# VectorE in place of GpSimd for the low parts of a feed-forward layer's weights

## The chip, the cores and the metric

The kernel runs on one core of a Trainium2 chip. The metric is the device time of one execution in microseconds (us); less is better. Three runs of the kernel before gave 726.19, 727.13 and 728.55 us, so the median is 727.13.

The engines are named as the profile names them: PE is TensorE's matmul, PEld its weight load, DVE is VectorE, ACT is ScalarE, POOL is GpSimd, SP is SyncE, whose queue issues nearly all DMAs.

## The reference

Three layers follow each other on 2 x 576 = 1152 tokens of width 512, all in float32:

```python
x = gate * memory(q) + (1 - gate) * causal_attention(q, k, v)   # 8 heads of 64
r = np.maximum(x @ w_in, 0.0); x = (r * r) @ w_out              # 512 -> 2048 -> 512
p = domain_probs / domain_probs.sum(-1, keepdims=True)
out = sum(p[:, e:e+1] * (np.maximum(x @ w1[e], 0.0) @ w2[e]) for e in range(4))
```

The first feed-forward layer (`w_in`, `w_out`) is the one that the change touches.

## The kernel before, in words

**Tiles and chunks.** The 1152 tokens are nine tiles of 128. The attention and the first feed-forward layer go through them in three chunks (`CHUNKS`, L38): chunk 0 has two tiles, chunk 1 four (512 columns), chunk 2 three (384 columns). The chunks of the layer overlap with the attention of what comes later: while the layer works on chunk 0 the attention of chunk 1 runs beside it, while it works on chunk 1 the attention of chunk 2 runs beside it (`mix`, L822; in the profile about 100 to 281 us), and while it works on chunk 2 (about 281 to 362 us) the weights and tokens of the experts are prepared (L1013 to L1027). Then come the experts, to the end.

**The weights of the layer.** `convert` writes the layer's weights into a DRAM buffer `w1s` during chunk 0: 16 blocks `f`, each with a half 0 (of `w_in`) and a half 1 (of `w_out`), 128 x 512 float32 each. Chunks 1 and 2 read all 32 halves back, each chunk for itself. To keep precision every product is made of three passes (`PASS`, L41): a weight is split into a high part in the narrower format `F32R` and a low part, the rest. High times high, high times low and low times high are added up.

**One block, step by step.** `prep(f, half)` (L725) does this for chunks 1 and 2: `fetch` (L719) sees to it that a DMA of the half into a tile `wraw` is under way (L723, three buffers); `split` (L82) makes the high part with a copy on ScalarE (L83), and the low part as `raw` minus the high part (L84), on VectorE or on GpSimd; then `fetch(2)` asks for the next half. The engine of L84 is chosen at L735: in chunk 1, VectorE makes half 0 of blocks 0 to 2 and half 1 of blocks 3, 7, 11 and 15; in chunk 2 half 1 of the odd blocks. That is 15 of 64; GpSimd makes the other 49, 25 in chunk 1 and 24 in chunk 2.

`up(f)` (L740) multiplies the tokens by half 0 (L106, 12 matmuls into `hpb` in chunk 1, `hpc` in chunk 2), then ScalarE takes the relu (L745), VectorE multiplies it by the same bank again, which gives the square `r` (L746), ScalarE copies its high part (L751) and VectorE makes its low part `g` (L752). `down(f)` (L755) multiplies by half 1 (L762, 12 matmuls). The loop (L774) preps half 0 of block f+1 and half 1 of block f-1, then runs `up(f)` and `down(f-2)`. In chunk 1 all `up` write into one bank but for one block, so the next `up` waits until L746 has read it; chunk 2 has two banks.

**What lies beside it.** In chunk 1 `attention_b` gives VectorE most of its work: L189 (masked scores and their maximum), L573 and L574 (the exponential's bias), L588 and L589 (high and low part of the exponentials), L511, L516, L530, L183 and L184 (keys, queries and values in parts). GpSimd makes the other keys' low parts (also L511). In chunk 2 VectorE has L873 and L890 (the experts' tokens) and L928 (the experts' weights), and GpSimd L931 to L936 (sums of the experts' weights). ScalarE also takes the squares of the experts' weights (L869), and SP issues their loads (L917).

**What sets the order.** The program order of PE is fixed by the source. The queues of the other engines are put in order by the framework's planner, from the program order and from when it expects each operand to be ready. Each engine works through its queue in that order.

Of the kernel before, what the change touches and what calls it, by code (L numbers as in the profile page):

```python
# [52 lines left out]
def attention_then_experts(ctx, tc, qa, ka, va, qc, kc, vc, mz, beta, w1, probs, w2, out):  # L53
# [11 lines left out]
    nc = tc.nc  # L65
# [16 lines left out]
    def split(w, raw, eng):  # L82
        nc.scalar.activation(out=w[:, 0], in_=raw, func=AF.Copy)  # L83
        eng.tensor_sub(w[:, 1], raw, w[:, 0].bitcast(F32))  # L84

    def y_of(c):

        t0 = CHUNKS[c][0]
        if t0 < LAST and 0 not in ys:
            ys[0] = xyp.tile([P, NK, LAST * P], F32, tag=f"x{c}", name="y0")  # L90
        e = int(t0 >= LAST)
        t0 -= EXPERT_CHUNKS[e][0]
        return ys[e][:, :, t0 * P:t0 * P + (CHUNKS[c][1] - CHUNKS[c][0]) * P]
# [3 lines left out]
    def mm_in(c, acc, w):  # L97
        i = 0
        for kk in range(NK):
            if c == 0:  # L100
                nc.tensor.matmul(
                    acc, lhsT=w[:, kk * P:(kk + 1) * P], rhs=first_x[:, kk, :],
                    start=(kk == 0), stop=(kk == NK - 1),
                )
            for a, b in PASS if c else ():
                nc.tensor.matmul(  # L106
                    acc, lhsT=w[:, a, kk * P:(kk + 1) * P], rhs=xs_r[c][:, b, kk, :],
                    start=(i == 0), stop=(i == 3 * NK - 1),
                )
                i += 1  # L110
            yield
# [598 lines left out]
    def ffn1(c, ps, gp, nh, cv=None):  # L710
        t0, t1 = CHUNKS[c]
        n = (t1 - t0) * P
        per = 512 // n
        gs, ws = {}, {}

        todo = [x for g in range(n1 + 1) for x in ((g, 0), (g - 2, 1)) if 0 <= x[0] < n1] + [(n1 - 1, 1)]
        raws = {}

        def fetch(ahead):  # L719
            while c and todo and len(raws) < ahead:  # L720
                x = todo.pop(0)
                raws[x] = wrp.tile([P, DM], F32, tag="wraw", name="wraw")
                nc.sync.dma_start(out=raws[x], in_=w1s[x])  # L723

        def prep(f, half):  # L725
            if c == 0:
                while (f, half) not in made:
                    next(cv)
                ws[f, half] = made.pop((f, half))
                next(cv, None)  # L730
                return
            fetch(1)
            raw = raws.pop((f, half))
            w = wp.tile([P, 2, DM], F32R, tag=f"w{half}", name=f"w{half}")
            on_vector = ((f < 3, f % 4 == 3), (False, f % 2))[c - 1][half]  # L735
            split(w, raw, nc.vector if on_vector else nc.gpsimd)
            ws[f, half] = w
            fetch(2)

        def up(f):  # L740
            spare = c == 1 and f == 1
            hp = (ps if spare or f % nh else ps_h).tile([P, n], F32, tag="s" if spare else "h", bufs=2 if spare else 1, name="hp" + "abc"[c])
            yield from mm_in(c, hp, ws.pop((f, 0)))
            r = gp.tile([P, n], F32, tag="r", name="r") if c else gp.tile([P, n], F32, tag="g", name="g0", bufs=3)
            nc.scalar.activation(out=r, in_=hp, func=AF.Relu)  # L745
            nc.vector.scalar_tensor_tensor(out=r, in0=hp, scalar=0.0, in1=r, op0=ALU.max, op1=ALU.mult)  # L746
            if c == 0:
                gs[f] = r
                return
            g = gp.tile([P, 2, n], F32R, tag="g", name="g", bufs=3)  # L750
            nc.scalar.activation(out=g[:, 0], in_=r, func=AF.Copy)  # L751
            nc.vector.tensor_sub(g[:, 1], r, g[:, 0].bitcast(F32))  # L752
            gs[f] = g

        def down(f):  # L755
            w, g = ws.pop((f, 1)), gs.pop(f)
            for d in range(NK):
                first, last = f == 0 and d % per == 0, f == n1 - 1 and d % per == per - 1
                if c == 0:
                    nc.tensor.matmul(yacc[d], lhsT=w[:, d * P:(d + 1) * P], rhs=g, start=first, stop=last)  # L760
                for i, (a, b) in enumerate(PASS if c else ()):
                    nc.tensor.matmul(  # L762
                        yacc[d], lhsT=w[:, a, d * P:(d + 1) * P], rhs=g[:, b],
                        start=(first and i == 0), stop=(last and i == 2),
                    )
                for k in range(d - per + 1, d + 1) if last else ():
                    nc.scalar.activation(out=y_of(c)[:, k], in_=yacc[k], func=AF.Copy)
                yield

        prep(0, 0)  # L770
        ps = (yield) or ps
        banks = [ps.tile([P, per, n], F32, tag=f"y{d}", name=f"y{d}") for d in range(NK // per)]
        yacc = [banks[d // per][:, d % per, :] for d in range(NK)]
        for f in range(n1 + 2):  # L774
            if f + 1 < n1:
                prep(f + 1, 0)
            if 1 <= f <= n1:
                prep(f - 1, 1)
            if f < n1:
                yield from up(f)  # L780
            if f >= 2:
                yield from down(f - 2)
        for k in range(NK):
            junk = gp.tile([P, n], F32, tag="r", name="junk")
            nc.scalar.activation(out=junk, in_=y_of(c)[:, k], func=AF.Square, accum_out=ysq[:, c, k:k + 1])
# [382 lines left out]
```

## Time and profile before

| what | before |
|---|---|
| median of three runs | 727.13 us |
| the profiled execution's own time | 726.71 us |
| its span, first to last instruction | 724.9 us |
| PE busy | 679.4 us (94%) |
| VectorE busy | 548.1 us (76%) |
| ScalarE busy | 428.2 us (59%) |
| GpSimd busy | 239.3 us (33%) |
| mean granted clock of TensorE | 0.991 of full speed |

The profile is of one execution; its span is 1.8 us shorter than that execution's own time. Busy time is what the engine's instructions took; the share is of the span. A line such as L84 is a line of the kernel. A busy PE isn't PE at its peak, since matmuls are pipelined and their ends modelled.

### The profile page before, as it was taken

Reading aid. Unit: us, or ns where it says so; the run is one execution under the profiler, and the core shown is the slowest. Engines: PE = TensorE matmul, PEld = TensorE weight load, DVE = VectorE, ACT = ScalarE, POOL = GpSimd, SP = SyncE. Lnnn points to the kernel's source line nnn. Section 1 sums busy time; section 2 is a strip of 40 time slices with the busy share of each in tenths; the row PEclk is TensorE's granted clock in tenths of the full one; section 3 lists DMA queues with packets and bytes.
Section 4 is the critical chain, followed back from the end, with each engine's and each line's share of the span. In section 5 each row is a group of like instructions: output and inputs, shape, how many; then the busy total and the mean of one; then the engine's idle time right before and its main releaser. Section 6 shows DMA issues by size and latency. Waiting matters only on the chain.

```text
span 724.9 us, 12553 instructions
## 1 busy us (share of the span) xinstructions
PE 679.4 (94%) x4604; PEld 482.5 (67%) x4604; DVE 548.1 (76%) x1058; ACT 428.2 (59%) x842; POOL 239.3 (33%) x247
## 2 busy tenths in 40 slices
PE   7799899988999999989899999999999999999997
PEld 4577677766777778989665655666655555555553
DVE  7888776499979853667788778998787785867763
ACT  5888894666665546877786667455544343535340
POOL 1011003245242365545524423544332323242400
PEclk9999999999999999999999999999999999999999
DMA  8987983468875554875321322333333131100002
GB/s 304 343 312 234 305 259 91 172 214 208 192 172 118 126 108 125 284 247 156 103 89 59 117 84 92 117 117 117 115 118 117 60 113 62 59 1 1 1 1 72
DMA packets 65422, 101.25 MB, mean 140 GB/s; under 512 B 32656, under 2 KB 34704, under 8 KB 65360
## 3 DMA queue, kind: packets, MB, share of 16 engines
q1 hardware_dynamic: 65216, 100.45, 45.2%
q8 instruction: 36, 0.59, 0.3%
q14 instruction: 26, 0.21, 0.1%
q10 hardware_dynamic: 144, 0.00, 0.0%
HBM read 82.87 MB, written 10.75 MB: 129 GB/s over the span
## 4 chain that ended last, share of the span: by engine, by line
PE 51%; DVE 19%; ACT 12%; DMA 7%; issue 6%; POOL 3%; SPq 0%; DVEq 0%; ACTq 0%; POOLq 0%
PE o L1056 19%; PE pe L964 16%; DMA raw<-in_w 4%; PE y L762 4%; PE hpb L106 3%; PE y L760 2%; PE pv L619 2%; ACT a L319 2%; DMA wraw<-w1s 2%; DVE wu L928 2%; DVE g L752 1%; DVE a L189 1%; DVE w L873 1%; PE sc L551 1%; DVE g L980 1%
## 5 line engine op out<-in xcount | busy, mean ns | idle before, releaser
L1056 PE MATMUL o<-w,g 128*128 128x512 f16 x864 | 218.3, 379 | 6.9 <-DVE g L980 3.6
L964 PE MATMUL pe<-xs,wu 128*128 128x256 f16 (+1 forms) x1344 | 196.3, 286 | 1.9 <-DVE h L985 1.9
L964 PEld LDWEIGHTS <-wu 128*128 128x128 f16 x1344 | 131.0, 98 | 69.9 <-issue 3.5
L1056 PEld LDWEIGHTS <-g 128*128 128x128 f16 x864 | 83.8, 98 | 77.2 <-DVE g L980 6.6
L84 POOL TENSOR_TENSOR w<-wraw,w 128x512 fp32r<-128x512 f32 x49 | 72.5, 1484 | 144.6 <-ACT w L83 144.2
L979 ACT ACTIVATE g<-h 128x512 f16<-128x512 f32 (+1 forms) x64 | 43.3, 677 | 105.7 <-DVE h L985 105.7
L762 PE MATMUL y<-g,w 128*128 128x512 f32 (+1 forms) x384 | 90.7, 372 | 1.7 <-ACT w L83 0.9
L994 POOL TENSOR_TENSOR u<-u,p 128x256 f32<-128x256 f32 (+1 forms) x32 | 32.4, 1012 | 131.9 <-ACT p L993 111.0
L762 PEld LDWEIGHTS y<-g,w 128*128 128x128 f32 x384 | 68.2, 189 | 9.9 <-ACT w L83 1.2
L980 DVE SCALAR_TENSOR_TENSOR g<-h,g 128x512 f16<-128x512 f32 (+1 forms) x64 | 50.5, 788 | 25.5 <-ACT g L979 25.2
L985 DVE SCALAR_TENSOR_TENSOR h<-pe,u 128x256 f32<-128x256 f32 (+1 forms) x96 | 42.9, 452 | 19.8 <-PE pe L964 15.7
L106 PE MATMUL hpb<-x,w 128*128 128x512 f32 x192 | 53.2, 414 | 4.7 <-DVE r L746 4.6
L931 POOL TENSOR_TENSOR ws<-raw 128x256 f32<-128x256 f32 x32 | 23.3, 728 | 102.0 <-issue 79.8
L928 DVE SCALAR_TENSOR_TENSOR wu<-ws,wpow,wu 128x512 f16<-128x512 f32 x64 | 50.9, 835 | 2.9 <-ACT wu L939 2.9
L873 DVE SCALAR_TENSOR_TENSOR w<-raw,wpow,w 128x512 f16<-128x512 f32 x64 | 48.1, 755 | 0.7 <-ACT w L872 0.6
L83 ACT ACTIVATE w<-wraw 128x512 fp32r<-128x512 f32 x64 | 39.6, 622 | 14.9 <-DMA wraw<-w1s 8.4
L869 ACT ACTIVATE junk<-raw 128x1024 bf16<-128x1024 f32 x32 | 33.6, 1050 | 20.6 <-DMA raw<-in_w 20.5
L106 PEld LDWEIGHTS hpb<-x,w 128*128 128x128 f32 x192 | 36.3, 196 | 13.7 <-DVE r L746 6.5
L872 ACT ACTIVATE w<-raw,wpow 128x512 f16<-128x512 f32 x64 | 44.6, 709 | 0.9 <-PE o L1056 0.9
L106 PE MATMUL hpc<-x,w 128*128 128x384 f32 x192 | 37.9, 341 | 4.0 <-POOL w L84 3.1
L189 DVE CUSTOM_DVE_ANT_0 a<-sc,mask 128x384 f32<-128x384 f32 (+4 forms) x80 | 35.7, 477 | 5.5 <-PE sc L551 5.1
L752 DVE TENSOR_TENSOR g<-r,g 128x512 fp32r<-128x512 f32 (+1 forms) x32 | 30.7, 961 | 10.4 <-ACT g L751 9.8
(169 smaller groups left out, 1164.4 us busy)
## 6 DMA issues: line engine op xcount, KB each, us to landing
raw<-in_w SPq DMA_DIRECT2D x64, 512.0 KB, 3.4
w<-in_w SPq DMA_DIRECT2D x32, 512.0 KB, 5.3
wraw<-w1s SPq DMA_DIRECT2D x64, 256.0 KB, 3.0
w1s<-bits SPq DMA_DIRECT2D x32, 256.0 KB, 3.2
kraw<-in_kc SPq DMA_DIRECT2D x8, 576.0 KB, 4.1
vraw<-in_vc SPq DMA_DIRECT2D x8, 320.0 KB, 4.1
qraw<-in_qc SPq DMA_DIRECT2D x4, 512.0 KB, 4.7
out<-acc SPq DMA_DIRECT2D x8, 256.0 KB, 2.1
```

Of the source, the lines that this page charges most:

```text
L84: eng.tensor_sub(w[:, 1], raw, w[:, 0].bitcast(F32))
L106: nc.tensor.matmul(acc, lhsT=w[:, a, kk * P:(kk + 1) * P], rhs=xs_r[c][:, b, kk, :], start=(i == 0), stop=(i == 3 * NK - 1),)
L189: nc.vector.tensor_tensor_reduce(out=dst, in0=sc, in1=msk, op0=ALU.add, op1=ALU.max, scale=1.0, scalar=-3.0e38, accum_out=m)
L762: nc.tensor.matmul(yacc[d], lhsT=w[:, a, d * P:(d + 1) * P], rhs=g[:, b], start=(first and i == 0), stop=(last and i == 2),)
L872: nc.scalar.activation(out=w0, in_=x, func=AF.Copy, scale=s)
L873: nc.vector.scalar_tensor_tensor(out=w1, in0=x, scalar=s, in1=w0, op0=ALU.mult, op1=ALU.subtract)
L928: nc.vector.scalar_tensor_tensor(out=w[:, 1, ks], in0=x, scalar=s1, in1=w[:, 0, ks], op0=ALU.mult, op1=ALU.subtract)
L964: nc.tensor.matmul(acc, lhsT=w[:, wa, k, kk * P:kk * P + P], rhs=x[:, xb, kk], start=(m == 0), stop=(m == 5))
L979: nc.scalar.activation(out=g[:, 0], in_=hm, func=AF.Relu)
L980: nc.vector.scalar_tensor_tensor(out=g[:, 1], in0=hm, scalar=0.0, in1=g[:, 0], op0=ALU.max, op1=ALU.subtract)
L985: nc.vector.scalar_tensor_tensor(out=out, in0=acc, scalar=HID, in1=x, op0=ALU.mult, op1=ALU.add)
L1056: nc.tensor.matmul(outs[t], lhsT=g[:, gb, r:r + P], rhs=w[:, wa], start=(p == 0 and m == 1 and k == 0), stop=(p == 3 and m == 0 and k == 2),)
```

## The change

All 64 subtractions of L84 go to VectorE, whatever the chunk, block and half. Nothing else is edited.

```diff
             w = wp.tile([P, 2, DM], F32R, tag=f"w{half}", name=f"w{half}")
-            on_vector = ((f < 3, f % 4 == 3), (False, f % 2))[c - 1][half]
-            split(w, raw, nc.vector if on_vector else nc.gpsimd)
+            split(w, raw, nc.vector)
             ws[f, half] = w
```

## Rows read from the trace of the kernel before

**Rows 1.** Busy time by stretch: window, length, busy per engine (instructions), PE's clock, DMA share, GB/s

```profile
140.00:190.00 50.00, 43.75 (x229) 34.05 (x228) 47.91 (x66) 32.99 (x60) 26.35 (x16) 0.93 0.82 220
190.00:250.00 60.00, 58.70 (x455) 46.09 (x454) 52.20 (x95) 34.57 (x73) 19.88 (x14) 1.00 0.66 146
281.00:322.00 41.00, 37.76 (x209) 35.73 (x210) 25.66 (x40) 35.15 (x71) 19.34 (x15) 1.00 0.77 263
```

**Rows 2.** The same stretches, L84 alone: VectorE, then GpSimd

```profile
140.00:190.00 50.00, 0.69 (x1) 16.24 (x10) 0.93 0.82 220
```

**Rows 3.** Line L84 in the whole run: shortest, median, longest ns, first and last start

```profile
L84 POOL TENSOR_TENSOR w<-wraw,w x49: 1276/1301/2507, 110.1 to 351.2; 128x512 fp32r<-128x512 f32 x49
L84 DVE TENSOR_TENSOR w<-wraw,w x15: 678/693/1532, 106.0 to 356.8; 128x512 fp32r<-128x512 f32 x15
```

**Rows 4.** Instructions in order of time, chunk 1: start, duration, engine, line

```profile
145.36 1.69 POOL L84 TENSOR_TENSOR w<-wraw,w 128x512 fp32r<-128x512 f32 x1 [1.31 <-ACT w L83]
145.84 1.76 DVE L752 TENSOR_TENSOR g<-r,g 128x512 fp32r<-128x512 f32 x1
...
148.25 4.62 PE L106 MATMUL hpb<-x,w 128*128 128x512 f32 x12 [3.44 <-DVE r L746]
...
187.39 0.68 DVE L752 TENSOR_TENSOR g<-r,g 128x512 fp32r<-128x512 f32 x1
```

**Rows 5.** Groups by line and form, VectorE, 140 to 250 us: count, busy us, mean ns

```profile
L752 DVE TENSOR_TENSOR g<-r,g 128x512 fp32r<-128x512 f32 x14 | 15.0, 1072 | 2.2 <-ACT g L751 2.2
L589 DVE TENSOR_TENSOR al<-a,ah 128x1024 f16<-128x1024 f32 x7 | 12.6, 1806 | 0.0
...
L573 DVE TENSOR_TENSOR mx<-mx 128x2 f32<-128x2 f32 x3 | 1.7, 569 | 0.1
```

**Rows 6.** Three VectorE lines in the whole run: shortest, median, longest ns

```profile
L589 DVE TENSOR_TENSOR al<-a,ah x12: 1212/1358/2345, 163.7 to 267.6; 128x1024 f16<-128x1024 f32 x8, 128x1152 f16<-128x1152 f32 x4
L573 DVE TENSOR_TENSOR mx<-mx x4: 161/163/1382, 177.6 to 262.4; 128x2 f32<-128x2 f32 x4
L746 DVE SCALAR_TENSOR_TENSOR r<-hpb,r x16: 677/686/694, 137.4 to 268.8; 128x512 f32<-128x512 f32 x16
```

**Rows 7.** Groups by line and form, GpSimd, 140 to 250 us

```profile
L84 POOL TENSOR_TENSOR w<-wraw,w 128x512 fp32r<-128x512 f32 x21 | 31.8, 1513 | 59.7 <-ACT w L83 59.4
L511 POOL TENSOR_TENSOR kst<-kraw,kst 64x576 fp32r<-64x576 f32 x8 | 14.5, 1827 | 14.1 <-ACT kst L509 12.6 <-issue 1.4
```

**Rows 8.** Groups by line and form, VectorE and GpSimd, 281 to 362 us

```profile
L752 DVE TENSOR_TENSOR g<-r,g 128x384 fp32r<-128x384 f32 x16 | 13.3, 832 | 7.5 <-ACT g L751 6.9 <-PE wt L851 0.6
L84 DVE TENSOR_TENSOR w<-wraw,w 128x512 fp32r<-128x512 f32 x8 | 7.8, 980 | 4.3 <-ACT w L83 4.1
...
L84 POOL TENSOR_TENSOR w<-wraw,w 128x512 fp32r<-128x512 f32 x21 | 29.6, 1422 | 34.0 <-ACT w L83 34.0
```

**Rows 9.** Waits: PE 140 to 285 us; PE 284 to 400; SP 284 to 345 (total, times, longest)

```profile
PE hpb L106 <- DVE r L746: 4.6, 2, 3.4
...
PE hpc L106 <- POOL w L84: 3.1, 4, 1.2
...
PE y L762 <- POOL w L84: 0.7, 1, 0.7
...
SPq L723 <- POOL w L84: 32.4, 18, 4.0
```

**Rows 10.** Instructions in order of time, chunk 2: two of PE's waits for GpSimd's L84

```profile
306.84 1.28 POOL L84 TENSOR_TENSOR w<-wraw,w 128x512 fp32r<-128x512 f32 x1 [2.71 <-ACT w L83]
...
307.45 1.21 DVE L84 TENSOR_TENSOR w<-wraw,w 128x512 fp32r<-128x512 f32 x1 [1.10 <-ACT w L83]
...
308.17 2.02 PE L106 MATMUL hpc<-x,w 128*128 128x384 f32 x10 [0.74 <-POOL w L84]
...
312.42 0.68 DVE L890 TENSOR_TENSOR tt<-y 128x512 f32<-128x512 f32 x1
...
314.28 2.00 PE L106 MATMUL hpc<-x,w 128*128 128x384 f32 x10 [1.18 <-POOL w L84]
```

## The prediction

> **What bounds the kernel now.** Read first the table of busy time by stretch, to see which engine is full where the change acts. It acts in two places. From 140 to 250 us the first layer's chunk 1 runs beside the attention of chunk 2. There VectorE is busy 47.9 of the first 50 us, while PE has 43.8; in the next 60 us PE has 58.7 and VectorE 52.2 [rows 1]. So VectorE sets the pace first, PE later. From 281 us on, in chunk 2, VectorE is busy only 25.7 of 41 us and PE 37.8 [rows 1]: there PE waits for operands. Read second the waits. Up to 285 us PE waits 4.6 us for L746, a VectorE instruction, and never in the leading rows for GpSimd's L84; after 284 us it waits 3.1 + 0.7 = 3.8 us, five times, for L84 on GpSimd [rows 9]. So the moved work is off PE's path in chunk 1 and on it in chunk 2.
>
> Read third what GpSimd does to VectorE. In order of time, at 145.36 us an L84 begins on GpSimd and runs 1.69 us; L752, begun beside it on VectorE, takes 1.76 us, where the same instruction took 0.68 us at 187.39 [rows 4]. The one is stretched by 1.08 us. L746 is not: its longest is 694 ns against 677 for its shortest [rows 6]. It is the one that reads one of its inputs from PE's bank.
>
> **The change, part by part.** *Which instructions move.* 49 subtractions leave GpSimd, 15 are on VectorE already [rows 3]. By time, 10 of the 49 lie between 140 and 190 us [rows 2], 21 between 140 and 250 [rows 7], 21 between 281 and 362 [rows 8]; the other seven lie around these, where I cost them at nothing: of what is left of chunk 1, VectorE's work is the thin end. One costs 0.69 us on VectorE, the median, against 1.30 on GpSimd [rows 3]. No DMA moves: the loads of `wraw` stay in SP's queue, in the same order.
>
> *What VectorE gains and loses in chunk 1.* Added: 21 x 0.69 = 14.5 us. Taken away: the stretch. In the groups of VectorE between 140 and 250 us, eleven have a mean far over their own fastest. The first is L752, 14 x (1.072 - 0.68) = 5.5 us [rows 4, 5]; the second L589, 7 x (1.806 - 1.212) = 4.2 [rows 5, 6]; the last L573, 3 x (0.569 - 0.161) = 1.2 [rows 5, 6]. With the eight between (L589's wider form, L530, L511, L574, two forms of L588, L184, L516), each against its own fastest, it comes to some 23 us. GpSimd spends 31.8 us of that stretch in L84 and 14.5 in L511 [rows 7], and L511 stays. By these shares 31.8 / 46.3 x 23 = 15.8 us would go. VectorE's net is 14.5 - 15.8 = -1.3 us. As VectorE is full for less than half of the stretch, I take 0 on the path. The bounds: nothing comes back, which puts 10 x 0.69 = 6.9 us on the path where VectorE is full; or all of it comes back early enough to take away PE's 4.6 us of waits for L746.
>
> A rule speaks against this move. The Trainium skill, in "Perfetto Trace Analysis", section Optimizing Scalar/DVE Operations, says that work may be offloaded from a saturated VectorE, even to GpSimd, but that the two share a read port, so that moving work between them might not help. By its first half the sum would be 726.7 + 6.9 - 2.7 = 730.9 us, by its second the term of chunk 1 is about nothing. The stretched L752 [rows 4] speaks for the second half.
>
> *What PE gains in chunk 2.* Five waits, 3.8 us [rows 9]. In the first one shown, L84 starts on GpSimd at 306.84 and ends at 308.12; VectorE is idle until 307.45 and could end it at 306.84 + 0.69 = 307.53, which saves 0.6 us. In the second, VectorE is in L890 until 313.10 and would end at 313.79, where PE went on at 314.28: 0.5 us [rows 10]. At 0.55 us each the five give 2.7 us. The bounds are nothing and the whole 3.8.
>
> *What VectorE bears in chunk 2.* Added 21 x 0.69 = 14.5 us. Its own eight L84 now take 0.980 us on the mean, against 0.678 at the fastest, so 2.4 us come back there [rows 3, 8]. L752 takes 0.832 on the mean [rows 8]; it is 384 columns wide and so should take under 0.6 (an estimate from the 0.68 at 512 [rows 4]), which gives another 16 x 0.23 = 3.7. The net is about +8.4 us. It is covered by 41 - 25.7 = 15.3 us in which VectorE is idle in the first part of this chunk alone [rows 1]. Without that cover it would cost the 8.4.
>
> *What comes earlier.* SP waits 32.4 us, 18 times, for L84 on GpSimd before it can issue the next `wraw` load [rows 9], since L84 is the last reader of that buffer. A shorter L84 lets it go sooner. I give that nothing, because DMAs are already busy 0.77 of the time in that stretch [rows 1]; it may help to make the 2.7 us stick.
>
> *The sum.* The profiled execution took 726.7 us (span 724.9, 1.8 around it); 726.7 + 0 - 2.7 = 724.0. The median of the runs is 0.4 above that execution, so 724.4 us, 0.37% less. About 0.3%, or 2.2 us, is what a measurement of this kernel can tell from no change.
>
> **The rivals.** *No difference that shows.* In chunk 2 each L84 stands behind a ScalarE copy and a DMA. VectorE's own L84 waited 4.1 us for L83 there [rows 8], and ScalarE is at 35.2 of 41 us [rows 1]. If PE's five waits pass to those, perhaps 0.7 us is left: 726.0, or 726.4 at the median. Against it: in the rows PE stands still to the end of GpSimd's own instruction.
>
> *Slower: the subtraction blocks VectorE's queue.* GpSimd now waits 59.4 us for L83 between 140 and 250 us and 34.0 after 281 [rows 7, 8]; it has little behind. On VectorE what stands behind is L746, for which PE already waits up to 3.4 us [rows 9]. The eight L84 of chunk 2 on VectorE had 4.3 us of idle time before them, 0.54 each [rows 8]. At half of it, 21 x 0.27 = 5.7 us come into chunk 1, less the 1.3 of relief 4.4, and in chunk 2 the full 0.54 eats the 0.55 saved. This gives 726.7 + 4.4 = 731.1, or 731.5 at the median. It turns the sign from (1.3 + 2.7) / 42 = 0.1 us per subtraction. The trace doesn't show where the planner will put the 42. PE's clock, 0.93 in the first 50 us and 1.00 after [rows 1], could add to it, as the stretch with PE's longest waits is the slow one. Against it: a full VectorE is late, and by then the copy is mostly done.
>
> *Slower: the stretch doesn't come back.* If what stretches VectorE's instructions is mostly L511, which stays on GpSimd, the 6.9 us of added work lie on the path from 140 to 190 us: 726.7 + 6.9 - 2.7 = 730.9, or 731.3 at the median. It turns the sign if less than 6.9 - 2.7 = 4.2 us is returned there. Against it: L84, not L511, is what runs beside the stretched L752 [rows 4]. The Trainium skill's first half, above, would make this the case.
>
> *Much faster.* The relief comes where VectorE is full: the 4.6 us of PE's waits for L746 go too, with all 3.8: 726.7 - 8.4 = 718.3, or 718.7.
>
> *The change does nothing* can't be: `split` is called from the edited line alone.
>
> **How the numbers follow.** Faster by over 0.3%: 0.42, of it 0.32 the forecast and 0.10 the large gain. No difference: 0.27. Slower by over 0.3%: 0.31, of it 0.21 the blocked queue and 0.10 the stretch that stays. The likeliest case's own range is 722.5 to 725. The range goes from 719.0, near the large gain, to 732.0, just over the slow case; some 0.05 lie below and 0.12 above.
>
> **What the profile after would show.** L84 x64 on VectorE, mean under 0.8 us, none on GpSimd. Busy time of VectorE near 548 + 49 x 0.69 - 15.8 - 6.1 = 560 us, or a little less, that of GpSimd down by over 61 (31.8 + 29.6, the two stretches) [rows 7, 8]. L752 at 512 columns near 0.7 to 0.8 us on the mean between 140 and 250. No wait of PE for GpSimd in chunk 2, and in its place waits for VectorE's L84 of under 1.5 us. I am wrong if PE's waits for L746 grow, if VectorE waits over 4 us for L83 between 140 and 250, or if PE's idle time in chunk 2 goes to `wraw` loads or ScalarE.

## The result, and the profile after

The changed kernel takes 718.59 us at the median of six runs, against 727.84 us for the kernel before in the same comparison: a ratio of 0.988, 95% interval 0.986 to 0.9901, or 9.25 us less. The profile after spans 716.8 us (before 724.9). The forecast was 724.4 us, 2.7 less, in a range from 719.0 to 732.0: the sign was right, the size under a third of what came, and the time lies just below the range. Two executions of the experiments were far slower, one of e5 (974.19 us) and one of e8 (1738.85 us); no ratio below counts them, the two medians do.

The edit is one line shorter, so from there on a line of the kernel before has a number lower by one: L745 in the profile after is L746 of before, L751 is L752. A line of three dots stands for lines of the view that are left out.

Busy time by stretch after, with the columns of [rows 1]:

```profile
140.00:190.00 50.00, 45.56 (x249) 35.24 (x249) 48.34 (x79) 36.60 (x66) 12.07 (x6) 1.00 0.86 234
190.00:250.00 60.00, 58.56 (x454) 46.18 (x452) 53.66 (x110) 35.13 (x74) 3.86 (x3) 1.00 0.65 151
281.00:322.00 41.00, 40.25 (x230) 39.29 (x230) 30.87 (x57) 36.37 (x73) 3.97 (x4) 1.00 0.81 278
```

Against [rows 1]: VectorE is as full as it was in the first stretch, 48.3 against 47.9 us, though it now carries all the subtractions. PE is busy 1.8 us more there and its clock is 1.00, not 0.93. From 281 us PE is busy 2.5 us more.

The groups of VectorE between 140 and 250 us, as in [rows 5]:

```profile
L84 DVE TENSOR_TENSOR w<-wraw,w 128x512 fp32r<-128x512 f32 x25 | 17.5, 708 | 0.0
L751 DVE TENSOR_TENSOR g<-r,g 128x512 fp32r<-128x512 f32 x14 | 11.7, 835 | 1.4 <-ACT g L750 1.2
...
L589 DVE TENSOR_TENSOR al<-a,ah 128x1024 f16<-128x1024 f32 x8 | 9.8, 1221 | 0.0
```

L589 is back near its fastest, 1.212 us [rows 6], with a mean of 1.221 against 1.806; L751 has 0.835 against 1.072. The last column says that VectorE's idle time before the 25 subtractions is 0.0 us in all.

Where the time went is best told by milestones: the first `hpb` matmul begins chunk 1, the first `hpc` matmul begins chunk 2, the first `hpc` matmul of block 15 its end, and the second L980 (L979 after) completes the experts' first hidden part. The rows, before and then after:

```profile
133.56 3.78 PE L106 MATMUL hpb<-x,w 128*128 128x512 f32 x15
...
280.85 0.44 PE L106 MATMUL hpc<-x,w 128*128 128x384 f32 x1 [0.38 <-ACT x L222]
...
344.65 0.51 PE L106 MATMUL hpc<-x,w 128*128 128x384 f32 x2
...
363.70 0.69 DVE L980 SCALAR_TENSOR_TENSOR g<-h,g 128x512 f16<-128x512 f32 x1
```

```profile
135.73 1.50 PE L106 MATMUL hpb<-x,w 128*128 128x512 f32 x5
...
278.95 0.44 PE L106 MATMUL hpc<-x,w 128*128 128x384 f32 x1 [0.32 <-ACT x L222]
...
339.90 2.24 PE L106 MATMUL hpc<-x,w 128*128 128x384 f32 x12
...
355.38 0.69 DVE L979 SCALAR_TENSOR_TENSOR g<-h,g 128x512 f16<-128x512 f32 x1
```

The same for every kernel of this study, in us, from its own profile:

| kernel | start of chunk 1 | chunk 1 | chunk 2, blocks 0 to 14 | end of chunk 2 | rest | span |
|---|---|---|---|---|---|---|
| before | 133.6 | 147.3 | 63.8 | 19.7 | 360.5 | 724.9 |
| after | 135.7 | 143.2 | 60.9 | 16.2 | 360.8 | 716.8 |
| e8, after again | 133.9 | 143.8 | 62.1 | 16.2 | 360.6 | 716.6 |
| e1, chunk 1 only | 135.5 | 142.5 | 62.4 | 18.7 | 360.7 | 719.8 |
| e2, chunk 2 only | 134.3 | 149.1 | 60.6 | 16.2 | 360.9 | 721.0 |
| e3, six subtractions in chunk 1 | 135.1 | 147.4 | 64.3 | 18.9 | 361.1 | 726.8 |
| e4, stretch put back | 134.7 | 157.7 | 66.0 | 21.0 | 360.2 | 739.6 |
| e5, last blocks of chunk 2 | 135.4 | 148.8 | 63.3 | 16.6 | 360.3 | 724.4 |
| e6, sums on VectorE | 133.8 | 147.2 | 65.6 | 16.3 | 361.7 | 724.6 |
| e7, keys on VectorE too | 134.0 | 147.1 | 60.0 | 16.2 | 362.1 | 719.4 |
| e9, GpSimd busy, not reading | 137.1 | 144.0 | 61.7 | 16.9 | 360.8 | 720.5 |
| e10, stretch back in chunk 1 | 133.5 | 151.7 | 60.4 | 16.2 | 360.3 | 722.0 |
| e11, keys on GpSimd | 133.6 | 147.7 | 60.5 | 16.2 | 359.9 | 717.9 |

So the change brings three things: chunk 1 is shorter by 4.1 us, the body of chunk 2 by 2.9, its end by 3.6; the 2.2 us that the profile after loses ahead of chunk 1 didn't come again in e8. The forecast had the middle one alone. How far the parts repeat can be read from the kernels that share a part. Chunk 1 takes 147.2 to 149.1 us in the four that leave it as it was (before, e2, e5, e6), and 142.5 to 143.8 in the three that change it as the change does (after, e8, e1). The body of chunk 2 takes 62.4 to 64.3 us as it was (before, e1, e3) and 60.6 to 62.1 changed (after, e8, e2), which nearly touch; its end 18.7 to 19.7 and 16.2.

**Chunk 1 in the order of time.** VectorE at the place of [rows 4], before: these two stand between an L746 and the L752 shown there. Then VectorE after, with PE's next start:

```profile
143.65 1.02 DVE L511 TENSOR_TENSOR kst<-kraw,kst 64x576 fp32r<-64x576 f32 x1
144.69 1.23 DVE L516 TENSOR_TENSOR qh<-qraw,qh 128x1024 fp32r<-128x1024 f32 x1
```

```profile
145.13 0.69 DVE L745 SCALAR_TENSOR_TENSOR r<-hpb,r 128x512 f32<-128x512 f32 x1
145.73 0.68 DVE L84 TENSOR_TENSOR w<-wraw,w 128x512 fp32r<-128x512 f32 x1
146.45 0.76 DVE L511 TENSOR_TENSOR kst<-kraw,kst 64x576 fp32r<-64x576 f32 x1
147.24 0.69 DVE L751 TENSOR_TENSOR g<-r,g 128x512 fp32r<-128x512 f32 x1
147.84 0.69 DVE L745 SCALAR_TENSOR_TENSOR r<-hpb,r 128x512 f32<-128x512 f32 x1
148.44 0.68 DVE L84 TENSOR_TENSOR w<-wraw,w 128x512 fp32r<-128x512 f32 x1
149.04 1.22 DVE L516 TENSOR_TENSOR qh<-qraw,qh 128x1024 fp32r<-128x1024 f32 x1
```

```profile
148.58 1.65 PE L106 MATMUL hpb<-x,w 128*128 128x512 f32 x6 [1.58 <-DVE r L745]
```

Between one L746 and the next, for which PE waits, VectorE had 1.02 + 1.23 + 1.76 = 4.0 us of work before. After, between the same two (L745 there), it has 0.68 + 0.76 + 0.69 = 2.1 us. Of the 1.9 us, 1.07 are the stretch of L752, beside which GpSimd's L84 ran [rows 4], and 0.26 that of L511. The remaining 0.55 are order: the planner moved L516, of 1.23 us, behind the second L745 and put one L84 of 0.68 in. VectorE is as full as it was, but less of its work stands ahead of the instruction that PE needs. PE's wait falls from 3.44 us [rows 4] to 1.58, and PE's clock stays up. The clock before, from 150 to 160 and from 180 to 190 us, and after, from 150 to 160:

```profile
150.00:160.00 10.00, 10.00 (x40) 7.75 (x40) 9.90 (x13) 6.31 (x10) 6.65 (x4) 0.86 0.59 180
...
180.00:190.00 10.00, 7.90 (x49) 6.31 (x50) 8.88 (x12) 7.01 (x17) 3.58 (x3) 0.83 1.00 218
```

```profile
150.00:160.00 10.00, 10.00 (x46) 7.67 (x44) 10.00 (x16) 7.84 (x13) 4.97 (x2) 1.00 0.64 216
```

Before, each low window follows a wait of PE, of 3.44 us up to 148.25 [rows 4] and of 2.1 us up to 182.1. A mean of 0.86 over 10 us is 0.14 x 10 / 0.5 = 2.8 us at 1.2 GHz and the rest at 2.4. The block after the first wait, from one first matmul to the next, took 8.39 us before and 6.76 after. So of chunk 1's 4.1 us, 1.85 are the shorter wait and 1.6 this block; the rest is small changes of either sign. The whole of chunk 1, before and then after:

```profile
133.56:280.85 147.29, 138.39 (x990) 109.33 (x988) 117.81 (x195) 86.81 (x179) 65.65 (x43) 0.98 0.67 165
```

```profile
135.73:278.95 143.22, 135.57 (x990) 106.93 (x988) 118.68 (x221) 86.81 (x179) 26.62 (x17) 1.00 0.68 171
```

PE stands idle 147.29 - 138.39 = 8.9 us before and 7.7 after, so its waits shrink by only 1.2 us in all. The other 2.8 us are the same matmuls done in less busy time, with the clock at 1.00 on the mean and not 0.98. This repeats: in the four kernels that leave chunk 1 as it was the clock's mean over it is 0.97 to 0.98, in after, e8, e1 and e9 it is 1.00.

**The end of chunk 2.** Before, in the order of time, on three engines:

```profile
343.89 1.60 POOL L84 TENSOR_TENSOR w<-wraw,w 128x512 fp32r<-128x512 f32 x1
...
345.44 1.19 POOL L932 TENSOR_TENSOR ws<-ws,raw 128x256 f32<-128x256 f32 x1
...
346.71 0.74 POOL L936 TENSOR_TENSOR ws<-raw,ws 128x256 f32<-128x256 f32 x1
...
347.48 1.15 ACT L939 ACTIVATE wu<-ws,wpow 128x1024 f16<-128x1024 f32 x1 [2.71 <-POOL ws L936]
...
350.55 0.62 ACT L83 ACTIVATE w<-wraw 128x512 fp32r<-128x512 f32 x1
...
351.22 0.96 PE L762 MATMUL y<-g,w 128*128 128x384 f32 x2 [0.92 <-ACT w L83]
```

It reads as one chain. The sums L932 and L936 stand behind L84 in GpSimd's queue; ScalarE's L939 waits 2.71 us for them, and with it all of ScalarE's queue; so the copy L83 of the last weights is late, and PE waits for it. After, the same two instructions of ScalarE:

```profile
339.51 1.15 ACT L938 ACTIVATE wu<-ws,wpow 128x1024 f16<-128x1024 f32 x1 [0.87 <-POOL ws L935]
...
342.58 0.62 ACT L83 ACTIVATE w<-wraw 128x512 fp32r<-128x512 f32 x1
```

L83 comes 342.58 - 339.90 = 2.7 us after the last block's start, where it came 350.55 - 344.65 = 5.9 us after it.

PE's waits in the body of chunk 2, as in [rows 9]:

```profile
PE hpc L106 <- DVE w L84: 0.5, 2, 0.3
```

Of the 3.1 us of PE's waits for L84 that stood there, 0.5 are left (0.9 in e8).

### The profile page after: what moved, and what is told of

Its sections match the earlier page's. It is cut to its first block, busy times and chain, and to the rows that moved or that the text cites. A ratio compares the mean times of both kernels' runs of the same rounds, so it can differ in the third digit from the quotient of the medians.

```text
span 716.8 us, 12523 instructions
## 1 busy us (share of the span) xinstructions
PE 676.4 (94%) x4604; PEld 480.9 (67%) x4604; DVE 553.3 (77%) x1107; ACT 428.0 (60%) x842; POOL 168.9 (24%) x198
## 4 chain that ended last, share of the span: by engine, by line
PE 36%; DVE 8%; DMA 3%; ACT 2%; issue 2%; POOL 1%; DVEq 0%; ACTq 0%; SPq 0%; POOLq 0%
PE o L1055 19%; PE pe L963 16%; DMA raw<-in_w 3%; DVE wu L927 2%; DVE w L872 1%; DVE g L979 1%; DVE h L984 1%; ACT junk L868 1%; DVE xs L872 1%; ACT g L978 1%; ACT wu L932 0%; DVE acc L1068 0%; DVE u L984 0%; POOL u L993 0%; DVE w L84 0%
## 5 line engine op out<-in xcount | busy, mean ns | idle before, releaser
L979 DVE SCALAR_TENSOR_TENSOR g<-h,g 128x512 f16<-128x512 f32 (+1 forms) x64 | 50.5, 789 | 25.7 <-ACT g L978 25.5
L84 DVE TENSOR_TENSOR w<-wraw,w 128x512 fp32r<-128x512 f32 x64 | 47.8, 753 | 14.0 <-ACT w L83 13.9
L106 PE MATMUL hpb<-x,w 128*128 128x512 f32 x192 | 51.0, 401 | 4.2 <-DVE r L745 4.2
L83 ACT ACTIVATE w<-wraw 128x512 fp32r<-128x512 f32 x64 | 39.6, 624 | 14.8 <-DMA wraw<-w1s 7.4
L210 POOL TENSOR_TENSOR xm<-xm,cf 128x512 f32<-128x512 f32 x7 | 8.1, 1162 | 138.0 <-DVE cf L209 94.7
```

The source lines that it names most:

```text
L106: nc.tensor.matmul(acc, lhsT=w[:, a, kk * P:(kk + 1) * P], rhs=xs_r[c][:, b, kk, :], start=(i == 0), stop=(i == 3 * NK - 1),)
L979: nc.vector.scalar_tensor_tensor(out=g[:, 1], in0=hm, scalar=0.0, in1=g[:, 0], op0=ALU.max, op1=ALU.subtract)
```

## The experiments

Theory A: the gain has three parts of its own, as above, and what costs in chunk 1 is that GpSimd's reads stretch VectorE. Theory B: the planner made another order, and the engine of L84 has no part of its own. Theory C, on the end of chunk 2 alone: it is short only because all of chunk 2 ran ahead. Ratios are against the kernel before on the same chip. The diffs show what an experiment has in place of the line of the kernel before, those of e7 and e11 in place of the line of the change.

**e1 and e2: one chunk at a time.**

```diff
-            on_vector = ((f < 3, f % 4 == 3), (False, f % 2))[c - 1][half]
+            on_vector = c == 1 or ((f < 3, f % 4 == 3), (False, f % 2))[c - 1][half]
```

and with `c == 2` in e2.

> Chunk 1's 25 subtractions on VectorE, chunk 2 as before. Theory A (three parts: in chunk 1 VectorE is no longer stretched by L84 and PE's stall at 144 to 148 us shrinks, with the low clock after it; in chunk 2 PE waits less for L84; at the end of chunk 2 the sums L931 to L936 no longer stand behind L84 on GpSimd): by PE's matmul starts chunk 1 alone brought 4.1 us, so 3 to 5 us less than before, with the clock between 140 and 190 us at 1.00. Theory B (the gain is the planner's new order of the queues, and the engine of L84 has no part of its own): any value, the parts of e1 and e2 don't add up to the 9 us.

> Chunk 2's 24 subtractions on VectorE, chunk 1 as before. Theory A: 2.9 us for PE's waits for L84 and 3.6 us at the end of chunk 2, so 5.5 to 7 us less than before; 140 to 190 us as before, clock 0.93. Theory B: any value, not the rest of e1 to 9 us.

e1: 721.92 us, ratio 0.9941 (0.9921 to 0.9961). Chunk 1 takes 142.5 us, 4.8 less than before, with the clock at 1.00. e2: 722.88 us, ratio 0.996 (0.994 to 0.998). Chunk 2 with its end takes 60.6 + 16.2 = 76.8 us against 83.5, 6.8 less; but chunk 1, which it doesn't touch, took 1.8 us more, all of it at its end, after a wait of 1.44 us of PE up to 273.5 us and with a clock of 0.83 from 270 to 280. By stretches the parts come near the change's, 4.8 + 6.8 against 4.1 + 6.4; by medians they give 4.5 + 3.5 = 8.0 of 9.25. Theory A holds for the stretches and missed e2's total, 3.5 us where it gave 5.5 to 7.

**e3: six subtractions.** `(c == 1 and f < 5) or` stands ahead of the old rule.

> Only six more subtractions on VectorE: those of blocks 0 to 4 of chunk 1. Theory A, if the stall at 144 to 148 us and the low clock behind it are what chunk 1 loses: most of e1's gain, 2.5 to 4 us less than before. If the relief is spread evenly over the 25: 6/25 of 4.1, 1.0 us.

728.18 us, ratio 1.002 (1.0001 to 1.0039): a miss. The first wait falls as in the change (1.56 us), and block 4 starts 3.5 us sooner than before, counted from the start of chunk 1 (1.94 us sooner in the trace, and chunk 1 began 1.53 us later). Then it is given back: GpSimd's L84 of the later blocks stretch VectorE again, and the next long wait is longer, 2.90 us against 1.2 in the profile after, with the low clock behind it. A stretched instruction ahead of that wait (it runs beside an L84 that GpSimd starts at 181.12, and takes 0.75 us in the profile after), PE's start, and the window:

```profile
181.23 1.85 DVE L588 CAST ah<-a 128x1152 f16<-128x1152 f32 x1
```

```profile
185.69 1.65 PE L106 MATMUL hpb<-x,w 128*128 128x512 f32 x3 [2.90 <-DVE r L746]
```

```profile
180.00:190.00 10.00, 7.01 (x46) 5.25 (x47) 9.52 (x13) 4.38 (x12) 2.69 (x2) 0.83 0.92 246
```

So chunk 1's loss isn't tied to one place. That the relief must last as long as VectorE is full is a reading of this run, not shown by it: VectorE's order in e3 isn't that of the change either.

**e4: the stretch put back.** VectorE makes all low parts; beside them GpSimd does 49 subtractions of the same size that nobody reads.

```diff
+            split(w, raw, nc.vector)
+            ((f < 3, f % 4 == 3), (False, f % 2))[c - 1][half] or nc.gpsimd.tensor_sub(..., w[:, 0].bitcast(F32), w[:, 0].bitcast(F32))
```

The three dots stand for a spare tile.

> All 64 subtractions on VectorE, and GpSimd does 49 subtractions of the same size beside them whose result nobody reads (two reads of the high part into a spare tile). Theory A: VectorE's instructions are stretched again and L931 to L936 stand behind 49 instructions on GpSimd again; PE's direct wait for GpSimd's L84 stays away. So most of the gain is lost: VectorE carries 14.5 us more than before between 140 and 250 us, and the time is 725 to 735 us. Theory B, or if latency alone made the gain: 718 to 721 us.

741.37 us, ratio 1.0211 (1.0179 to 1.0244), beyond the upper end of what theory A gave. Chunk 1 takes 157.7 us. VectorE's groups between 140 and 250 us show why:

```profile
L752 DVE TENSOR_TENSOR g<-r,g 128x512 fp32r<-128x512 f32 x13 | 13.2, 1012 | 1.0 <-ACT g L751 0.8
...
L589 DVE TENSOR_TENSOR al<-a,ah 128x1024 f16<-128x1024 f32 x6 | 9.0, 1501 | 0.0
```

VectorE has the work and the stretch at once. In chunk 1 VectorE's 221 instructions and ScalarE's 178 stand in the same order as in the change, and ScalarE's L83 never waits for GpSimd there, so only GpSimd's subtractions differ. Beside them the durations of VectorE's 221 sum to 146.0 us, against 131.9 in e8, and PE's wait at the place of [rows 4] is nearly the old one again:

```profile
149.13 1.12 PE L106 MATMUL hpb<-x,w 128*128 128x512 f32 x2 [3.14 <-DVE r L746]
```

With the order held, the stretch alone raises this wait from 1.58 to 3.14 us. Theory B falls: the engine that makes the low part, and so the latency, is that of the change, the order in chunk 1 is too, and the time is 23 us longer.

**e9: GpSimd as busy, but not reading.** Instead of each unread subtraction, a copy of one column and two memsets.

```diff
+            if not ((f < 3, f % 4 == 3), (False, f % 2))[c - 1][half]:
+                ...
+                nc.gpsimd.tensor_copy(spare[:, 0:1], w[:, 0, 0:1].bitcast(F32))
+                nc.gpsimd.memset(spare, 0.0)
+                nc.gpsimd.memset(spare, 0.0)
```

> As e4, but GpSimd's 49 unread subtractions are each two memsets of 560 columns behind a copy of one column: GpSimd is as busy and stands as long before L511 and L931 to L936, and hardly reads SBUF. Theory A, with what e4 cost put down to the reads that VectorE's two-input instructions collide with: L752 at 512 columns under 0.8 us on the mean where e4 has 1.01, chunk 1 (first hpb matmul to first hpc matmul) 142 to 146 us where before has 147.3 and e4 157.7. As for the whole, 718 to 725 us. If it is GpSimd's time, whatever it does, that costs: 735 to 745 us as e4.

719.92 us, ratio 0.9903 (0.988 to 0.9926), and chunk 1 144.0 us. GpSimd's groups between 140 and 250 us, and two of VectorE's (its line of `g` is L756 here):

```profile
L740 POOL MEMSET spare<- 128x560 f32 x22 | 13.3, 606 | 1.3
L739 POOL MEMSET spare<- 128x560 f32 x22 | 12.5, 568 | 1.3
L738 POOL COPY spare<-w 128x1 f32<-128x1 f32 x22 | 11.2, 508 | 49.5 <-ACT w L83 49.1
```

```profile
L756 DVE TENSOR_TENSOR g<-r,g 128x512 fp32r<-128x512 f32 x14 | 11.7, 835 | 1.6 <-ACT g L755 1.4
...
L589 DVE TENSOR_TENSOR al<-a,ah 128x1024 f16<-128x1024 f32 x7 | 8.5, 1220 | 0.0
```

GpSimd is busier than in e4 (13.3 + 12.5 + 11.2 = 37.0 us against 26.9 of its unread subtractions), and VectorE's means are those of the change (0.835 and 1.220 us here, 0.835 and 1.221 there). VectorE's order in chunk 1 is that of the change for the first 207 of its 221 instructions, and the clock's mean over the chunk is 1.00, where e4 has 0.95. It isn't GpSimd's time that costs VectorE, it is what it reads. The Trainium skill, in "SBUF — State Buffer", section Who interferes with whom, says that a VectorE instruction with two SBUF inputs contends with a GpSimd instruction that reads SBUF and not with one that only writes it; e4 and e9 agree, by L752's 1.012 us against 0.835. The expected mean of L752 under 0.8 us was missed by little, because L511 still stretches it, as in the change.

**e10: the stretch in chunk 1 alone.** e4 with `c == 2 or` ahead of the condition of the unread subtraction.

> As e4, but with the unread subtractions in chunk 1 alone; chunk 2 is that of the change. Theory A: chunk 1 as in e4, 154 to 159 us, and chunk 2 (first hpc matmul to the end of the experts' first hidden part) 76 to 79 us as with the change: 725 to 734 us in all.

729.61 us, ratio 1.0025 (1.0001 to 1.0048). The profile is of the fastest of its twelve runs, 723.78 us; in it chunk 1 takes 151.7 us, under what was expected, and chunk 2 with its end 76.5 us, as with the change. At the median the run is 5.8 us longer than in its profile, which would bring chunk 1 to the expected 154 to 159, if the difference lies there; that wasn't measured.

**e5 and e6: the end of chunk 2.** e5 moves six subtractions, `(c == 2 and f > 11) or` ahead of the old rule. e6 leaves L84 as before and moves the sums of the first two pairs:

```diff
-        nc.gpsimd.tensor_add(s[:, 0], u[:, 0], u[:, 3])
+        (nc.vector if i < 2 else nc.gpsimd).tensor_add(s[:, 0], u[:, 0], u[:, 3])
```

and so for the other three.

> Only chunk 2's blocks 12 to 15 on VectorE besides what was there (six more subtractions). Theory A says that 3.6 us of the gain lie behind the last block's start, because ScalarE's L939 waits 2.7 us for the sum L936, which stands behind L84 on GpSimd: from the start of the last block's matmuls to the end of the experts' first hidden part before has 19.7 us, after 16.2; here 16 to 17, and 2.5 to 4 us less than before in all. Rival C (the end of chunk 2 is short only because all of chunk 2 ran ahead): 19 to 20 us there, no difference in all.

> L84 as before the change; only the sums L931 to L936 of the experts' first two weight blocks go to VectorE (eight instructions of 256 columns). Theory A: the sums no longer stand behind L84, so the same stretch falls from 19.7 to 16 to 18 us, 1.5 to 3.5 us less in all; PE's waits for L84 stay. Rival C: 19 to 20 us there and no difference.

The end of chunk 2 takes 16.6 us in e5 and 16.3 in e6, 16.2 after, 19.7 before. Either way of taking the sums out from behind L84 gives nearly the whole of it, 3.2 and 3.5 of 3.6 us, and in e6 L84 itself is untouched: theory C falls, and this part is GpSimd's queue. In all, e5 takes 723.92 us (0.9953, 0.9935 to 0.9971), e6 724.03 us (0.9967, 0.9951 to 0.9983). e6 lost 1.8 us in the body of chunk 2, where PE waited 1.8 us for ScalarE's L83 up to 313.15 us and its clock from 310 to 320 us was 0.68.

**e7 and e11: the other work that the two engines share.** In e7 all of L511 goes to VectorE besides the change, in e11 all of it to GpSimd:

```diff
-                    (nc.vector if b else nc.gpsimd).tensor_sub(k[64:128, js], ...)
+                    nc.vector.tensor_sub(k[64:128, js], ...)
```

and `nc.gpsimd` in e11.

> The change, and GpSimd's eight halves of L511 go to VectorE as well, so that nothing on GpSimd stretches VectorE between 140 and 210 us. VectorE gains 8 x 0.75 = 6.0 us of work and loses a stretch of some 8 us that L511 still makes after the change. Theory A: 0 to 2 us less than the change alone. If an empty GpSimd lane has a worth of its own (two engines side by side): 1 to 4 us more.

> The change, and VectorE's eight halves of L511 go to GpSimd, which then has 16: the reverse of e7. VectorE loses 7.2 us of work between 140 and 210 us, GpSimd takes 8 x 1.8 more. If VectorE's amount of work in chunk 1 sets the pace: 1 to 3 us less than the change. If GpSimd's reads cost VectorE as much as the work (0.7 us of stretch for each instruction beside it, as L84 did): within 2 us of the change. If the keys come too late from GpSimd (eight more behind each other, 1.8 us each): 2 to 5 us more.

> The changed kernel once more, for e7 to be compared with on one chip and to see whether the first 2.2 us that its profile lost before chunk 1 come again. If they are the program's: matmuls of chunk 1 begin 2 us later than before; if they are the run's: within 1.5 us of it, either way. Time 716 to 721 us.

On one chip e7 takes 721.86 us (ratio to before 0.9918, 0.989 to 0.9947) and the change (e8) 718.50 (0.9875, 0.9851 to 0.9899). So e7 is 3.4 us longer at the median, though the two intervals overlap a little, and though GpSimd does nothing at all beside chunk 1 up to 250 us. It starts better (PE's first wait is 0.8 us), then PE waits 3.0 us up to 193.53, and its clock from 190 to 200 us is 0.72. In that profile, ScalarE and then VectorE:

```profile
187.10 0.58 ACT L745 ACTIVATE r<-hpb 128x512 f32<-128x512 f32 x1
```

```profile
187.95 1.28 DVE L84 TENSOR_TENSOR w<-wraw,w 128x512 fp32r<-128x512 f32 x2
189.16 1.21 DVE L516 TENSOR_TENSOR qh<-qraw,qh 128x1024 fp32r<-128x1024 f32 x1
...
191.01 0.76 DVE L511 TENSOR_TENSOR kst<-kraw,kst 64x576 fp32r<-64x576 f32 x1
...
192.00 0.76 DVE L511 TENSOR_TENSOR kst<-kraw,kst 64x576 fp32r<-64x576 f32 x1
192.79 0.69 DVE L746 SCALAR_TENSOR_TENSOR r<-hpb,r 128x512 f32<-128x512 f32 x1
```

Here the order is the bad one: L746 could start when ScalarE is done at 187.68 and starts at 192.79, behind L84, L516 and two L511. This is what the prediction's slower rival feared, from other work than L84. e11 takes 720.26 us (0.9922, 0.9892 to 0.9953): within 2 us of the change, on the slower side. Ahead of PE's first long wait, of 2.84 us up to 147.75, stand two instructions of VectorE that GpSimd's L511 stretches:

```profile
142.84 2.45 DVE L516 TENSOR_TENSOR qh<-qraw,qh 128x1024 fp32r<-128x1024 f32 x1
145.21 1.88 DVE L752 TENSOR_TENSOR g<-r,g 128x512 fp32r<-128x512 f32 x1
```

In both, chunk 1 takes as long as before the change, 147.1 and 147.7 us, with the clock at 0.98 and 0.97 on the mean: its whole gain is lost again, though L84 is on VectorE. In e7 plain work stands ahead of L746, in e11 stretched work. So the gain of chunk 1 doesn't follow from the engine of L84 alone. Neither beats the change, which stays the fastest kernel here. In e8 chunk 1 begins at 133.9 us, as before: the 2.2 us that the first profile lost there belong to that run.

## Why the prediction was wrong, point by point

*Which stretch has which limit.* Right: VectorE full and PE short of it up to 190 us, PE waiting for GpSimd's L84 in chunk 2.

*VectorE's account in chunk 1.* The mechanism was right, and e4 and e9 show it. The sum, nearly nothing net, was right as well: VectorE's busy time from 140 to 250 us goes from 47.91 + 52.20 to 48.34 + 53.66 us, by +1.9 where -1.3 was forecast. The step that failed is the sentence that followed, "I take 0 on the path". A net of nothing on VectorE isn't nothing for PE: what counts is whether the loss stands ahead of L746 or behind it, and whether PE's clock falls after the wait. The chunk gained 4.1 us in the profile after, 3.5 in e8 and 4.8 in e1; of the 4.1, 1.2 are PE's idle time and 2.8 the clock, which the forecast had named for the slower side alone. The rival named "much faster" had this (the 4.6 us of PE's waits for L746), was given 0.10, and its 718.7 us is what came. Even that was right in its total rather than its working: PE's waits for L746 didn't go (4.2 us of 4.6 are left); the low clock went, and with it some of the other waits. Its total came by other terms, so it is luck that it fits.

*PE's five waits in chunk 2.* Right: 2.7 us forecast, 2.9 in the profile after, 1.7 in e8. PE waits 0.5 and 0.9 us for VectorE's L84 there, under the 1.5 of the forecast.

*What the forecast left out.* The second step that failed: the end of chunk 2 has no term in the sum, and it brought 3.6 us. "What comes earlier" looked at SP's queue alone, and not at what stands behind L84 in GpSimd's own queue: L931 to L936, ScalarE's L939 behind them, and ScalarE's next L83 behind that. The prediction knew of L931 to L936 and costed only L84's five direct waits.

*The rivals on the slower side.* The blocked queue: VectorE's idle time before the 25 subtractions from 140 to 250 us is 0.0 us, so no subtraction blocked the queue by waiting for its copy. The stretch that stays: it went, and e4 shows its price when it doesn't. The rule that was weighed, of the Trainium skill, "Perfetto Trace Analysis", section Optimizing Scalar/DVE Operations (offloading to GpSimd may help a saturated VectorE, but the two share a port): the second half decides, by chunk 1 of e1 (4.8 us less than before) and of e4 (14.4 us more than after).

*The details.* VectorE's busy time went to 553.3 us (560 forecast), GpSimd's from 239.3 to 168.9. The mean of L752 came to 0.835 us, over the 0.7 to 0.8 of the forecast.

Not settled: how much of chunk 1's gain is the order in which the planner put VectorE's instructions. At the place of [rows 4] it is 0.55 of 1.9 us; for the whole chunk it is open, since no run has the engines of the change in another order with nothing else changed.

## What to carry to other kernels

Before a two-input instruction on SBUF is left on GpSimd to spare a full VectorE, compare the mean of VectorE's instructions beside it with their fastest: here the 26 unread subtractions beside chunk 1 of e4 cost VectorE 14.1 us, 0.54 each, where doing one on VectorE takes 0.69. When an instruction leaves an engine's queue, list everything that stood behind it on that engine and follow it two engines on, not only its own readers. And an account that nets to nothing on one engine still has to be placed: ahead of the instruction that PE waits for, or behind it.

## What the runs showed of the hardware that was not expected

Waits of PE of the same length were followed by a low clock in one run and not in another. In e2 the clock from 270 to 280 us was 0.83 after a wait of 1.44 us; in the profile after, with a wait of 1.45 us at the same place, it was 1.00. First e2, then after:

```profile
270.00:280.00 10.00, 8.56 (x81) 6.96 (x81) 4.52 (x8) 2.48 (x6) 5.34 (x5) 0.83 0.37 85
```

```profile
270.00:280.00 10.00, 8.93 (x89) 6.96 (x89) 3.66 (x5) 5.24 (x13) 3.17 (x3) 1.00 0.26 76
```

And a copy of a single column on GpSimd took 0.51 us on the mean beside a full VectorE (e9), nearly as long as a memset of 560 columns, 0.57 to 0.61.
